# Row sums of an attention kernel gathered in two sets of heads instead of four, with a fourth sum tile and seven weight tiles

## The chip, the core and the metric

The program runs on one core of a Trainium2 chip. Its engines work side by side and meet only through semaphores: PE (TensorE, matmuls; PEld is its weight load), DVE (VectorE, elementwise work), ACT (ScalarE, activations, and here also copies out of PSUM), POOL (GpSimd, which here issues DMAs) and SP (SyncE, which issues most DMAs). The metric is the device time of the whole program in microseconds (us), lower is better. Before the change it is 1789.01 us, the median of three runs (1788.33 to 1789.2).

## What is computed

Two blocks work on the same 2048 tokens of width 1024 and are mixed by a gate for each token. Block A is attention with 32 heads of width 32; block B is a mixture of 64 small experts picked by product keys. The change touches block A only, and there the sum under the softmax:

```python
def _A_ref(x, wqkv, wo):
    qkv = (x @ wqkv) ...                      # q, k, v: 32 heads, 32 wide
    scores = einsum("bhqd,bhkd->bhqk", q, k) * (Dh ** -0.5)
    p = _softmax(scores, axis=-1)
    o = einsum("bhqk,bhkd->bhqd", p, v)
    return o.transpose(...).reshape(B, S, D) @ wo

g = sigmoid((x * gate_w).sum(-1, keepdims=True))
return g * a + (1 - g) * b
```

The kernel divides late. It multiplies the exponentials with V as they are, sums them over the keys beside that, and scales the heads' outputs by gate over sum ("scale factors") just before the product with `wo`.

## The kernel before

**Stages.** The first third computes q, k, the experts' scores and v. Attention follows, from about 606 to 1611 us. The product with `wo` and the experts' part end the program.

**Steps.** Attention runs over 32 heads (`H`) with 16 tiles of 128 keys each (`NT`); one tile of one head is a step, numbered `16 * head + tile`. A loop takes two steps at a time, as a batch: scores of two tiles on PE (`scores`, eight matmuls of 512 columns into a ring of seven PSUM banks), their exponentials on ACT into a tile P of 128 keys by 2048 queries, then the products P times V of the two tiles before (`pv`). After that come the functions that `at(step, ...)` has put down for these steps, and then `presum` of the two new tiles. The order on each engine's queue is this written order; SP and POOL too work their queues in order, so a DMA that waits holds what stands behind it.

**Where the sums come from.** A head's exponentials are summed over tiles first. DVE adds most tiles P into a sum tile `ACC[h]` (`presum`, L1449 and L1451). One tile of each head, `ACCD[h]`, takes up two or three others by accumulating DMAs that POOL issues (L1444). `merge` (L1454) adds both, five steps into the next head. That leaves 128 rows. For heads 0 to 27 accumulating DMAs from POOL fold them: `fold_half` to 64 rows, `fold_quarter` to 32, and for heads 0 to 23 `fold_eighth` to 16. `gather` (SP) moves the rows left to the head's place in a tile F of 128 rows. When a set of heads is complete (0 to 7, 8 to 15, 16 to 23 with 16 rows each, 24 to 27 with 32 each), `group_sums` does four matmuls with a selector (`sel8` or `sel`) into one ring bank, evicts them with ACT (L1484) and stores one row of sums per head with a DMA each (`smd<-ssb` in the profile). The heads 28 to 31 are summed by PE one by one (`head_sums`, and at the end L1739).

**Scale factors.** For each group of four heads `load_r` loads the sums (`rr<-smd`), `norm_r` makes their reciprocals and multiplies by the gate on DVE (L1517, L1518) and stores them (`rd<-rr`), all on SP's queue. `load_rb` later loads them spread out, for the first 256 tokens (`RB[0]`, tile `rb0`) and the next (`RB[1]`).

**Memory.** P has eight places, planned ahead in `p_places`: a place is held for 5 steps where DVE reads the tile and for 9 where a DMA does. A write to a place waits for the last reader of the tile that stood there. Four places lie in a pool on the left side of the memory, four on the right. `ACC` has three tiles, used in turn; the third shares its place with `vhl`, which is loaded near the end.

**The end of attention.** In head 31 (steps 496 to 511) `split_first` prepares the first operands of the product with `wo` on ACT and DVE between the exponentials and the sums. Then `merge(31)`, `rowsum` of head 31 (L1739) and its way through DRAM to the scale factors of the last group run, while PE does the products for which factors are there (`wo_mm`).

Of the kernel before, what the change touches and what calls it, by code (L numbers as in the profile page):

```python
# [9 lines left out]
F32 = mybir.dt.float32  # L10
# [3 lines left out]
OP = mybir.AluOpType  # L14
AX = mybir.AxisListType

S = 2048
D = 1024
H = 32
KC = D // 128  # L20
HC = KC // 2
NT = S // 128
# [9 lines left out]
def gated_mha_peer_kernel(ctx, tc, xT, wqkv, wv, wo, wq, k12, ug, v, out):  # L32
# [8 lines left out]
    nc = tc.nc  # L41
# [24 lines left out]
    ident = const.tile([128, 128], F32, name="ident")  # L66
    ones = const.tile([128, 32], F32, name="ones")
# [5 lines left out]
    warm = const.tile([128, 112], F32, name="fill")  # L73
# [4 lines left out]
    def dma(dst, src, queue=nc.sync):  # L78
        a, b = (ap.bitcast(F32) if ap.dtype == F32R else ap for ap in (dst, src))
        return queue.dma_start(a, b)  # L80
# [343 lines left out]
    for kc in range(KC):  # L424
# [12 lines left out]
        order = [(w, n, i) for w in range(2) for i in range(3) for n in range(2)]  # L437
        if kc == 0:
            order = [(w, n, i) for n in range(2) for pair in ((0, 2), (1,)) for w in range(2) for i in pair]
        if kc == KC - 1:  # L440
            order = [(w, n, i) for w in range(2) for n in range(2) for i in range(3)]
# [227 lines left out]
    wl_, wh_, pools = [], [], []  # L669
# [33 lines left out]
    sel = const.tile([128, KC * 4], F32, name="sel")  # L703
# [554 lines left out]
    P, pools = {}, {}  # L1258
# [2 lines left out]

    def p_places():

        due, last, order = list(range(-8, 0)), [0] * 8, []
        for k in range(H * NT):
            h, kt = divmod(k, NT)
            if kt != SUMS[h][0]:
                i = min(range(8), key=lambda j: due[j])
                due[i], last[i] = k + (9 if kt in SUMS[h] else 5), k
                order.append(i)  # L1270
        by_last = sorted(range(8), key=lambda j: last[j])
        return iter([by_last.index(i) for i in order])

    def p_tile(h, kt):

        i = next(pools["places"])
        P[h, kt] = pools["left" if i >= 4 else "right"].tile([128, S], F32, name=f"P{i}")
        return P[h, kt]

    def first_scores(*banks):  # L1280

        tp.close()
        pools.update(right=Pool("ppr", side="right"), places=p_places())
        K, Q = Z
        for kt, places in enumerate(banks):
            pt = p_tile(0, kt)
            for qc, i in enumerate(places):
                ps = ps1.tile([128, 512], F32, name=f"bk{i}")
                c = slice(qc * 512, (qc + 1) * 512)
                nc.tensor.matmul(ps, K[:98, kt * 128:(kt + 1) * 128], Q[:98, c], start=True, stop=True)  # L1290
                nc.scalar.activation(pt[:, c], ps, AF.Exp, scale=SCALE)
# [29 lines left out]
    ACC = {}  # L1321

    def new_acc(h):
        if h % 3 == 2 and h < H - 2:
            ACC[h] = keep.tile([128, S], F32, name="vhl")
        else:
            ACC[h] = wk.tile([128, S], F32, name=f"acc{h % 3 if h < H - 2 else h % 2}", bufs=1)

    def load_vhl(i):
        if i == 0:  # L1330
# [7 lines left out]
    wk = Pool("wk", bufs=2)  # L1338

    new_acc(0)  # L1340
    nc.vector.memset(sel, 0.0)
    for i in range(4):
        nc.vector.memset(sel[32 * i:32 * i + 32, i:i + 1], 1.0)
    sel8 = warm[:, :32]
    nc.vector.tensor_reduce(sel8[:, :8], ident.rearrange("p (j r) -> p j r", j=8), axis=AX.X, op=OP.max)
    nc.vector.memset(sel8[:, 8:], 0.0)
    vpool = Pool("vpool", bufs=2)
    kq = Pool("kq")
    pools["left"] = Pool("ppl")
# [7 lines left out]
    ring = pss.tile([128, NB, 512], F32, name="ring")  # L1357
# [3 lines left out]
    def ring_banks(n):  # L1361
        i = [(ring_no[0] + k) % NB for k in range(n)]
        ring_no[0] += n
        return i

    def on_ring(ins, *banks):

        for other, theirs in users:
            if ins.ins.engine != other.ins.engine and not theirs & set(banks):
                tc.declare_no_dep(ins.ins, other.ins, reason="different banks of the ring")  # L1370
        users.append((ins, set(banks)))
        del users[:-6 * NB]
# [56 lines left out]

    def rowsum(ps, *srcs, by=ones):
        for src in srcs:
            for qc in range(NQ):
                yield nc.tensor.matmul(ps[32 * qc:32 * qc + 32, :], by,
                                       src[:, qc * 512:(qc + 1) * 512],
                                       start=(src is srcs[0]), stop=(src is srcs[-1]))

    def presum(h, kt):
        sums = SUMS[h]  # L1440
        if kt == 0 or kt == sums[0] or (h == H - 1 and kt == NT - 1):
            return
        if kt in sums:
            nc.gpsimd.dma_start(ACCD[h], P[h, kt], accum_op=OP.add)  # L1444
            return
        if kt == min(set(range(1, NT)) - set(sums)):
            if h > 0:
                new_acc(h)
            nc.vector.tensor_add(ACC[h], P[h, 0], P[h, kt])  # L1449
        else:  # L1450
            nc.vector.tensor_add(ACC[h], ACC[h], P[h, kt])  # L1451
# [4 lines left out]
    F = {}  # L1456
# [7 lines left out]
    def fold_eighth(h):  # L1464
        nc.gpsimd.dma_start(ACC[h][:16], ACC[h][16:32], accum_op=OP.add)

    NE = 24

    def set_of(h):
        return (h // 8 * 8, 8) if h < NE else (NE, 4)  # L1470

    def gather(h):
        first, n = set_of(h)
        if h == first:
            F[first] = keep.tile([128, S], F32, name="rb0")
        rows, j = 128 // n, h - first
        dma(F[first][rows * j:rows * j + rows], ACC.pop(h)[:rows])

    def group_sums(first, n):
        i, = ring_banks(1)  # L1480
        for ins in rowsum(ring[:, i, :], F.pop(first), by=sel8 if n == 8 else sel):
            on_ring(ins, i)
        o = wk.tile([128, 512], F32, name="ssb")
        on_ring(nc.scalar.activation(o, ring[:, i, :], AF.Copy), i)  # L1484
        for j in range(n):
            g, r = divmod(first + j, 4)
            dma(SMD[g][r:r + 1, :].rearrange("o (q s) -> (o q) s", q=NQ), o[j::32, :])

    def head_sums(h):
        i, = ring_banks(1)  # L1490
        for ins in rowsum(ring[:, i, :], ACC.pop(h)):
            on_ring(ins, i)
        on_ring(norm_sums(h, ring[:, i, :]), i)
# [71 lines left out]
    def at(step, f, *a):  # L1565
        todo.setdefault(step, []).append((f, a))

    for h in range(H):
        base = h * NT
        g, j = divmod(h, 4)  # L1570
        if h < H - 1:
            at(base + NT, finish, h)
            at(base + NT + 5, merge, h)
            if h >= NP:
                at(base + NT + 8, head_sums, h)
            else:
                at(base + NT + 9, fold_half, h)
                first, n = set_of(h)
                if n == 8:
                    at(base + 2 * NT, fold_quarter, h)  # L1580
                    at(base + 2 * NT + 7, fold_eighth, h)
                    at(base + 2 * NT + 12, gather, h)
                else:
                    at(base + 2 * NT + 4, fold_quarter, h)
                    at(base + 2 * NT + 8, gather, h)
                if h == first + n - 1:
                    step = base + (3 * NT + 4 if n == 8 else 2 * NT + 14)
                    at(step, group_sums, first, n)
                    for i in range(n // 4):
                        at(step + 6 + 6 * i, load_r, first // 4 + i)  # L1590
                        at(step + 10 + 6 * i, norm_r, first // 4 + i)
        if h >= 1 and h + 1 < H:
            at(base + 2, load_head, h + 1)
        if g + 1 < G:
            at(base + 7, load_v, g + 1, j)
# [6 lines left out]
        at(30 * NT + 9 + i, load_vhl, i)  # L1602
    at(29 * NT + 13, load_o, 0, 0, 4)
    at(30 * NT + 7, load_o, 0, 4, KC - 1)
    at(30 * NT + 13, load_rb, 0, 0, KC - 1)
    at((H - 1) * NT + 8, load_rb, 1, 0, KC - 1)


    BT = 2
# [127 lines left out]
    load_t(2, [zp.tile([128, S], F32R, name="z1")], [fin.tile([128, S], F32R, name="t3l")])  # L1737
    sm = pso.tile([128, 512], F32, name="o")
    list(rowsum(sm, P[H - 1, NT - 1], ACC.pop(H - 1)))  # L1739
    split_hi(1)  # L1740
    for kc in range(1, KC - 1):
# [169 lines left out]
```

## Time and profile before

| | us |
|---|---|
| median of 3 runs | 1789.01 |
| lowest, highest | 1788.33, 1789.2 |
| the profiled execution | 1789.59 |
| its span, first to last instruction | 1787.5 |
| PE, ACT and DVE busy in the 100 us from 1000 | 100.00, 98.32, 91.40 |

A profile is one execution. Rows of a timeline give the start and the duration in us, the engine, the line, what is written from what, and how many instructions were merged into the row; in square brackets stands the idle time of the engine ahead of it and what ended that. "PEld" rows are weight loads, which stand ahead of their matmuls; "SPq" rows are DMAs being issued on SP, so their duration is that of the issue and not of the transfer. A row of the windows view gives, for a stretch, its length and for PE, PEld, DVE, ACT and POOL the busy time with the count of instructions, then the granted clock (1.00 throughout), the share of the DMA engines and GB/s. The granted clock of the whole execution is 1.0.

### The profile page before, as it was taken

How to read it: one execution, taken by the hardware profiler on the slowest of the kernel's cores; microseconds unless marked ns; L12 is line 12 of the kernel's file. 1: busy time of each engine (PE TensorE's matmuls, PEld its weight loads, DVE VectorE, ACT ScalarE, POOL GpSimd, SP SyncE). 2: the span in 40 equal slices, each digit the busy share in tenths (PEclk: the TensorE clock that was granted, in tenths of full speed). 3: DMA queues.
4: the chain of work that ended last, by engine and by line, in shares of the span. 5: the costliest groups of instructions: out<-in, count | busy, mean ns of one | idle time of the engine just before them, and what ended most of it. 6: DMA issues, size and time to landing. Idle time of an engine off the chain costs nothing.

```text
span 1787.5 us, 26063 instructions
## 1 busy us (share of the span) xinstructions
PE 1782.3 (100%) x9871; PEld 1090.3 (61%) x9871; DVE 1513.2 (85%) x1309; ACT 1307.3 (73%) x1705; POOL 297.3 (17%) x439
## 2 busy tenths in 40 slices
PE   9999999999999999999999999999999999999999
PEld 7777777888888644444444444444444444447887
DVE  8866876779997898989899998989989898887874
ACT  6545544532453699999999999999999999994221
POOL 1222222244213101111111111111111110000000
PEclk9999999999999999999999999999999999999999
DMA  8887687361348669899999999998989897888541
GB/s 286 315 310 267 223 311 294 131 210 58 113 174 293 210 142 200 173 197 183 176 206 194 199 191 203 194 189 197 191 188 195 189 196 173 198 190 300 205 160 59
DMA packets 120167, 361.17 MB, mean 202 GB/s; under 512 B 17800, under 2 KB 51864, under 8 KB 97320
## 3 DMA queue, kind: packets, MB, share of 16 engines
q0 software_dynamic: 31808, 160.76, 40.2%
q1 hardware_dynamic: 87456, 197.55, 35.6%
q8 instruction: 78, 1.28, 0.3%
q10 hardware_dynamic: 776, 1.19, 0.2%
q14 instruction: 49, 0.40, 0.1%
HBM read 173.04 MB, written 72.36 MB: 137 GB/s over the span
## 4 chain that ended last, share of the span: by engine, by line
PE 97%; DMA 1%; DVE 1%; issue 0%; ACT 0%; DVEq 0%; SPq 0%; ACTq 0%
PE ring L1402 29%; PE o L1423 26%; PE bk L304 15%; PE bk L987 7%; PE pa L987 7%; PE bk L729 5%; PE bk L292 2%; PE bk L346 2%; PE bk L1003 1%; PE pa L1662 1%; DVE acc L1451 1%; DMA wo_raw<-t0l 0%; PE bk L194 0%; DMA smd<-ssb 0%; DMA rb<-rd 0%
## 5 line engine op out<-in xcount | busy, mean ns | idle before, releaser
L1412 ACT ACTIVATE P<-ring 128x1024 f32<-128x1024 f32 (+2 forms) x1027 | 910.6, 987 | 16.7 <-PE ring L1402 0.6
L1451 DVE TENSOR_TENSOR acc<-acc,P 128x2048 f32<-128x2048 f32 x230 | 527.1, 2292 | 34.9 <-ACT P L1412 14.5
L1423 PE MATMUL o<-P,V 128*32 128x512 f32 x3840 | 464.8, 599 | 0.0
L1402 PE MATMUL ring<-Q,K 98*128 98x512 f32 x1024 | 272.3, 408 | 0.0
L1402 PEld LDWEIGHTS ring<-Q,K 98*128 98x128 f32 x1024 | 182.0, 188 | 144.6 <-ACT P L1412 80.3
L1402 PE MATMUL ring<-z,z 98*128 98x512 f32 x1016 | 269.5, 407 | 0.0
L1402 PEld LDWEIGHTS ring<-z,z 98*128 98x128 f32 x1016 | 180.8, 188 | 141.5 <-ACT P L1412 79.9
L1451 DVE TENSOR_TENSOR vhl<-vhl,P 128x2048 f32<-128x2048 f32 x104 | 238.3, 2292 | 17.7 <-ACT P L1412 8.3
L1423 PEld LDWEIGHTS o<-P,V 128*32 128x32 f32 x3840 | 98.8, 109 | 223.1 <-issue 213.7
L1444 POOL DMA_DIRECT2D accd<-P x81 | 72.1, 890 | 772.5 <-ACT P L1412 558.4
L304 PE MATMUL bk<-xh,A 128*128 128x512 f32 x336 | 81.9, 394 | 0.0
L304 PE MATMUL bk<-xh,S 128*128 128x512 f32 x336 | 81.0, 392 | 0.0
L304 PE MATMUL bk<-xl,S 128*128 128x512 f32 x336 | 79.7, 389 | 0.0
L304 PEld LDWEIGHTS bk<-xh,A 128*128 128x128 f32 x336 | 62.2, 188 | 22.0 <-issue 2.5
L139 ACT ACTIVATE hi<-u 128x512 fp32r<-128x512 f32 x42 | 26.5, 632 | 65.3 <-DVE u L520 35.6
L1449 DVE TENSOR_TENSOR acc<-P,P 128x2048 f32<-128x2048 f32 x22 | 50.4, 2292 | 26.9 <-ACT P L1412 26.8
L304 PEld LDWEIGHTS bk<-xl,S 128*128 128x128 f32 x336 | 63.0, 188 | 13.1
L304 PEld LDWEIGHTS bk<-xh,S 128*128 128x128 f32 x336 | 62.6, 188 | 12.9
L987 PE MATMUL pa<-woh,acc 128*128 128x512 f32 x216 | 70.0, 389 | 0.0
L1412 ACT ACTIVATE accd<-ring 128x1024 f32<-128x1024 f32 (+2 forms) x64 | 62.2, 1030 | 0.1
L520 DVE TENSOR_TENSOR u<-u,bk 128x512 f32<-128x512 f32 x70 | 46.6, 683 | 5.6 <-DMA wpd<-u 4.9
L1454 DVE TENSOR_TENSOR acc<-acc,accd 128x2048 f32<-128x2048 f32 x22 | 50.3, 2285 | 0.0
(329 smaller groups left out, 2323.0 us busy)
## 6 DMA issues: line engine op xcount, KB each, us to landing
accd<-P POOLq DMA_DIRECT2D x81, 1024.0 KB, 10.1
wqt<-in_wq SPq DMA_DIRECT2D x48, 512.0 KB
wraw<-in_wqkv SPq DMA_DIRECT2D x28, 512.0 KB
acc<-acc POOLq DMA_DIRECT2D x19, 512.0 KB, 12.1
kd<-hi POOLq DMA_DIRECT2D x32, 256.0 KB, 3.6
kd<-lo POOLq DMA_DIRECT2D x32, 256.0 KB, 5.6
qd<-hi POOLq DMA_DIRECT2D x32, 256.0 KB, 3.4
qd<-lo POOLq DMA_DIRECT2D x32, 256.0 KB, 3.5
```

Of the source, the lines that this page charges most:

```text
L292: nc.tensor.matmul(b0[w, n], AW[PLAIN[w, ki]][a][:, k, :], X[f"B{ki + 1}{n + 1}"][b][:, k, :], start=first, stop=last)
L304: nc.tensor.matmul(ps, a[i][:, k, :], b[j][:, k, :], start=(k == 0 and i == j == 0), stop=(k == HC - 1 and i == 1))
L520: nc.vector.tensor_tensor(out=out, in0=a, in1=b, op=OP.add)
L729: nc.tensor.matmul(ps, x_part(a, t // 4, kc)[:, tok], b, start=first, stop=last)
L987: nc.tensor.matmul(ps, self.a[a][i][:, k, :], self.b[b][j][k], start=(not first and k == 0 and i == j == 0), stop=(k == HC - 1 and i == 1))
L1402: on_ring(nc.tensor.matmul(ring[:, i, :], K[:98, kt * 128:(kt + 1) * 128], Q[:98, qc * 512:(qc + 1) * 512], start=True, stop=True), i)
L1412: on_ring(nc.scalar.activation(P[h, kt][:, q0 * 512:(q0 + m) * 512].rearrange("p (a m) -> p a m", a=m), ring[:, i:i + m, :], AF.Exp, scale ...
L1423: nc.tensor.matmul(O[h][32 * qc:32 * qc + 32, :], Vt[g][:, kt, 32 * j:32 * j + 32], p[:, qc * 512:(qc + 1) * 512], start=(kt == 0), stop=( ...
L1444: nc.gpsimd.dma_start(ACCD[h], P[h, kt], accum_op=OP.add)
L1449: nc.vector.tensor_add(ACC[h], P[h, 0], P[h, kt])
L1451: nc.vector.tensor_add(ACC[h], ACC[h], P[h, kt])
L1454: nc.vector.tensor_add(ACC[h], ACC[h], ACCD[h])
```

## The change

Heads 0 to 15 form one set, folded to 8 rows each, and heads 16 to 27 the other, where 16 to 23 are folded to 8 rows and 24 to 27 to 16. Each set is summed in one go with a selector of its own. A new fold, `fold_sixteenth`, makes 8 rows of 16. The sets are summed at steps 301 and 484 (before: 164, 292, 420 and 478), and the loads and norm steps of the groups follow in turn, six steps apart: at 307 to 329 for the four groups of the first set, and for the three of the second the loads at 490, 496 and 502 and the norm steps at 494, 500 and 506 (before, the last norm step of these was at 488). The loads of the scale factors for the first tokens follow suit: `RB[0]` in two parts, at steps 493 and 509, and `RB[1]` at 511 instead of 504.

`ACC` gets a fourth tile, `acc3`, in the left pool, and P has seven places instead of eight, three of them on the left.

```diff
     def p_places():
-        due, last, order = list(range(-8, 0)), [0] * 8, []
+        due, last, order = list(range(-7, 0)), [0] * 7, []
...
-                i = min(range(8), key=lambda j: due[j])
+                i = min(range(7), key=lambda j: due[j])
...
-        P[h, kt] = pools["left" if i >= 4 else "right"].tile([128, S], F32, name=f"P{i}")
+        P[h, kt] = pools["right" if i in (0, 1, 4, 5) else "left"].tile([128, S], F32, name=f"P{i}")
...
     def new_acc(h):
-        if h % 3 == 2 and h < H - 2:
+        i = h % 4 if h < H - 2 else 3 if h == H - 2 else 1
+        if i == 2:
             ACC[h] = keep.tile([128, S], F32, name="vhl")
+        elif i == 3:
+            ACC[h] = pools["left"].tile([128, S], F32, name="acc3")
         else:
-            ACC[h] = wk.tile([128, S], F32, name=f"acc{h % 3 if h < H - 2 else h % 2}", bufs=1)
+            ACC[h] = wk.tile([128, S], F32, name=f"acc{i}", bufs=1)
...
-    nc.vector.memset(sel, 0.0)
-    for i in range(4):
-        nc.vector.memset(sel[32 * i:32 * i + 32, i:i + 1], 1.0)
-    sel8 = warm[:, :32]
-    nc.vector.tensor_reduce(sel8[:, :8], ident.rearrange("p (j r) -> p j r", j=8), axis=AX.X, op=OP.max)
-    nc.vector.memset(sel8[:, 8:], 0.0)
+    SETS = {0: (16, [8] * 16), 16: (12, [8] * 8 + [16] * 4)}
+    by = {0: sel, 16: warm[:, :32]}
+    nc.vector.tensor_reduce(sel[:, :16], ident.rearrange("p (j r) -> p j r", r=8), axis=AX.X, op=OP.max)
+    nc.vector.tensor_copy(by[16][:, :8], sel[:, :8])
+    nc.vector.tensor_reduce(by[16][:, 8:12], ident[:, 64:].rearrange("p (j r) -> p j r", r=16), axis=AX.X, op=OP.max)
+    nc.vector.memset(sel[:, 16:], 0.0)
+    nc.vector.memset(by[16][:, 12:], 0.0)
...
+    def fold_sixteenth(h):
+        nc.gpsimd.dma_start(ACC[h][:8], ACC[h][8:16], accum_op=OP.add)
...
     def gather(h):
-        first, n = set_of(h)
+        first, (r0, n) = set_of(h), rows_of(h)
         if h == first:
             F[first] = keep.tile([128, S], F32, name="rb0")
-        rows, j = 128 // n, h - first
-        dma(F[first][rows * j:rows * j + rows], ACC.pop(h)[:rows])
+        dma(F[first][r0:r0 + n], ACC.pop(h)[:n])
...
-                if n == 8:
-                    at(base + 2 * NT, fold_quarter, h)
-                    at(base + 2 * NT + 7, fold_eighth, h)
-                    at(base + 2 * NT + 12, gather, h)
-                else:
-                    at(base + 2 * NT + 4, fold_quarter, h)
-                    at(base + 2 * NT + 8, gather, h)
+                folds = {32: {36: fold_quarter}, 16: {32: fold_quarter, 39: fold_eighth},
+                         8: {32: fold_quarter, 39: fold_eighth, 46: fold_sixteenth}}[rows]
+                for step, f in folds.items():
+                    at(base + step, f, h)
+                at(base + {32: 40, 16: 44, 8: 53}[rows], gather, h)
                 if h == first + n - 1:
-                    step = base + (3 * NT + 4 if n == 8 else 2 * NT + 14)
+                    step = base + {32: 46, 16: 52, 8: 61}[rows]
...
-    at(30 * NT + 13, load_rb, 0, 0, KC - 1)
-    at((H - 1) * NT + 8, load_rb, 1, 0, KC - 1)
+    at(30 * NT + 13, load_rb, 0, 0, 4)
+    at((H - 1) * NT + 13, load_rb, 0, 4, KC - 1)
+    at((H - 1) * NT + 15, load_rb, 1, 0, KC - 1)
```

In `at(base + ..., gather, h)` and the lines around it `base` is `16 * h`, so a head's own steps run from `base` to `base + 15`.

More of the change, by code (lines that the diff above doesn't have):

```diff
@@ L1267, in p_places @@
             if kt != SUMS[h][0]:
-                i = min(range(8), key=lambda j: due[j])
+                i = min(range(7), key=lambda j: due[j])
                 due[i], last[i] = k + (9 if kt in SUMS[h] else 5), k
                 order.append(i)
-        by_last = sorted(range(8), key=lambda j: last[j])
+        by_last = sorted(range(7), key=lambda j: last[j])
         return iter([by_last.index(i) for i in order])
@@ L1424, in pv, with rowsum @@
                              p[:, qc * 512:(qc + 1) * 512], start=(kt == 0), stop=(kt == NT - 1))
-    def rowsum(ps, *srcs, by=ones):
+    def rowsum(ps, *srcs, w=ones):
         for src in srcs:
             for qc in range(NQ):
-                yield nc.tensor.matmul(ps[32 * qc:32 * qc + 32, :], by,
+                yield nc.tensor.matmul(ps[32 * qc:32 * qc + 32, :], w,
                                        src[:, qc * 512:(qc + 1) * 512],
@@ L1465, in fold_eighth, with rows_of @@
         nc.gpsimd.dma_start(ACC[h][:16], ACC[h][16:32], accum_op=OP.add)
-    NE = 24
+    def fold_sixteenth(h):
+        nc.gpsimd.dma_start(ACC[h][:8], ACC[h][8:16], accum_op=OP.add)
     def set_of(h):
-        return (h // 8 * 8, 8) if h < NE else (NE, 4)
+        return max(f for f in SETS if f <= h)
+    def rows_of(h):
+        first = set_of(h)
+        rows = SETS[first][1]
+        return sum(rows[:h - first]), rows[h - first]
     def gather(h):
-        first, n = set_of(h)
+        first, (r0, n) = set_of(h), rows_of(h)
         if h == first:
             F[first] = keep.tile([128, S], F32, name="rb0")
-        rows, j = 128 // n, h - first
-        dma(F[first][rows * j:rows * j + rows], ACC.pop(h)[:rows])
+        dma(F[first][r0:r0 + n], ACC.pop(h)[:n])
     def group_sums(first, n):
         i, = ring_banks(1)
-        for ins in rowsum(ring[:, i, :], F.pop(first), by=sel8 if n == 8 else sel):
+        for ins in rowsum(ring[:, i, :], F.pop(first), w=by[first]):
             on_ring(ins, i)
@@ L1577, in gated_mha_peer_kernel @@
                 at(base + NT + 9, fold_half, h)
-                first, n = set_of(h)
-                if n == 8:
-                    at(base + 2 * NT, fold_quarter, h)
-                    at(base + 2 * NT + 7, fold_eighth, h)
-                    at(base + 2 * NT + 12, gather, h)
-                else:
-                    at(base + 2 * NT + 4, fold_quarter, h)
-                    at(base + 2 * NT + 8, gather, h)
+                rows, first = rows_of(h)[1], set_of(h)
+                n = SETS[first][0]
+                folds = {32: {36: fold_quarter}, 16: {32: fold_quarter, 39: fold_eighth},
[3 more added lines that the diff above has]
+                at(base + {32: 40, 16: 44, 8: 53}[rows], gather, h)
                 if h == first + n - 1:
-                    step = base + (3 * NT + 4 if n == 8 else 2 * NT + 14)
+                    step = base + {32: 46, 16: 52, 8: 61}[rows]
                     at(step, group_sums, first, n)
```

## The prediction

> **What bounds the kernel.** I read the page first, then one stretch of its windows, then the chain and short timelines. The page's busy table and chain come first; the third row (windows view) is 100 us of attention.
>
> ```profile
> PE 1782.3 (100%) x9871; PEld 1090.3 (61%) x9871; DVE 1513.2 (85%) x1309; ACT 1307.3 (73%) x1705; POOL 297.3 (17%) x439
> ...
> PE 97%; DMA 1%; DVE 1%; issue 0%; ACT 0%; DVEq 0%; SPq 0%; ACTq 0%
> ```
>
> ```profile
> 1000.00:1100.00 100.00, 100.00 (x619) 46.78 (x612) 91.40 (x41) 98.32 (x115) 16.91 (x20) 1.00 0.94 197
> ```
>
> PE carries 97% of the chain, but in attention ACT is at 98.3% and DVE at 91.4%, so time taken from PE counts only as far as the other two follow. The chain, in order of time, shows the beat:
>
> ```profile
> 918.86 2.07 PE ring L1402 x8
> 935.32 2.07 PE ring L1402 x8
> 943.13 2.07 PE ring L1402 x8
> ```
>
> Two batches of two tiles take 943.13 - 935.32 = 7.81 us, so a step (one tile) is 1.953 us. From 918.86 to 935.32 are 16.46 us, four batches (15.62) and 0.84 more. The PE timeline there shows what the extra is, and the views of lines L1435 and L1484 how often:
>
> ```profile
> 924.75 1.92 PE L1423 MATMUL o<-P,V 128*32 128x512 f32 x16
> 926.49 1.04 PE L1435 MATMUL ring<-rb,fill 128*32 128x512 f32 x8
> 927.46 1.89 PE L1402 MATMUL ring<-z,z 98*128 98x512 f32 x7
> ```
>
> ```profile
> L1435 PE MATMUL ring<-rb,fill x24: 592/592/592, 926.5 to 1428.8; 128*32 128x512 f32 x24
> ...
> L1435 PE MATMUL ring<-rb,sel x8: 592/592/592, 1543.4 to 1543.8; 128*32 128x512 f32 x8
> ```
>
> ```profile
> L1484 ACT ACTIVATE ssb<-ring x4: 597/599/602, 927.6 to 1544.5; 128x512 f32<-128x512 f32 x4
> ```
>
> Four group sums stand in the path (24 records and 8, eight to a set), each 0.84 to 0.85 us of PE: the attention part is set by PE.
>
> The end of head 31 is another matter. There DVE runs without a pause behind the exponentials and PE waits for it (DVE's timeline, then PEld's):
>
> ```profile
> 1585.13 2.29 DVE L1449 TENSOR_TENSOR acc<-P,P 128x2048 f32<-128x2048 f32 x1 [3.86 <-ACT P L1412]
> ...
> 1594.48 7.08 DVE L1451 TENSOR_TENSOR acc<-acc,P 128x2048 f32<-128x2048 f32 x3
> 1601.47 1.22 DVE L1561 TENSOR_TENSOR z<-wo_raw,z 128x1024 fp32r<-128x1024 f32 x1
> ...
> 1612.45 2.29 DVE L1454 TENSOR_TENSOR acc<-acc,accd 128x2048 f32<-128x2048 f32 x1
> ```
>
> ```profile
> 1614.80 0.16 PEld L1435 LDWEIGHTS o<-acc,ones 128*32 128x32 f32 x8 [0.92 <-DVE acc L1454]
> 1615.79 0.77 PEld L1655 LDWEIGHTS pa<-woh,z 128*128 128x128 f32 x4 [0.84 <-ACT z L1683]
> ```
>
> DVE last waits for ACT at 1585.13; the merge of head 31 ends at 1614.74, and PE's sums of that head start at 1614.80. What follows hangs on that merge: the sums' way through DRAM, and PE's one later gap:
>
> ```profile
> 1640.06 1.20 PE L1655 MATMUL pa<-woh,z 128*128 128x512 f32 x4 [0.39 <-ACT z L98]
> ```
>
> **The change, part by part.** (1) *Two group sums instead of four.* Eight matmuls (16 records) and two evictions of 599 ns go. On PE that is 2 x 0.85 = **-1.70 us** up to head 31. The two evictions free ACT, which is not what ends there.
>
> (2) *Scale factors later.* The norm step (L1517, L1518) of groups 4 to 6 moves: the set of heads 16 to 27 is summed at step 484, so these steps fall on 494, 500 and 506, and the last two lie in head 31 (496 on), where before there was none. Before, the last was at step 488, in head 30; its price is in DVE's timeline:
>
> ```profile
> 1559.29 7.08 DVE L1451 TENSOR_TENSOR acc<-acc,P 128x2048 f32<-128x2048 f32 x3
> 1566.29 0.54 DVE L1517 RECIPROCAL rr<-rr 128x64 f32<-128x64 f32 x1
> 1566.87 0.22 DVE L1518 TENSOR_TENSOR rr<-rr,G 128x64 f32<-128x64 f32 x1
> 1567.01 2.29 DVE L1451 TENSOR_TENSOR acc<-acc,P 128x2048 f32<-128x2048 f32 x1
> ```
>
> Three adds take 7.08, so they start (7.08 - 2.29) / 2 = 2.395 apart, 0.10 more than one lasts: each needs its forerunner's result. The third starts at 1564.08 and the next add at 1567.01, 2.93 later: between two adds a norm step costs 0.53, because part of it fills that gap. Step 500 stands between two adds: 0.53. Step 506 stands before the subtractions of step 507, which fill the gap already (it starts at 1601.47, 0.09 ahead of the last add's end at 1601.56), so it costs its whole 1566.29 to 1567.01 = 0.72. Together **+1.25 us** on DVE after 1585.13. The bounds are 0, if something slower hid them, and 2 x 0.76 = 1.5, the two bare durations. Nothing in the rows hides them, so I take 1.25. Head 30 has one norm step before and after, and 3.86 us idle behind it.
>
> So DVE starts head 31 1.70 earlier and ends it 1.70 - 1.25 = 0.45 earlier; PE, free 1.70 earlier, waits 1.25 for the merge, and the rest moves with that.
>
> (3) *Seven places for P.* A place is taken again after at least 6 steps where DVE reads it (8 places gave one more) and 10 where a DMA does. The tightest kind is tile 14 of head 19, which would take the place of tile 8. DVE's rows (adds of tiles 5 on, then tile 8 alone) and ACT's:
>
> ```profile
> 1212.30 23.85 DVE L1451 TENSOR_TENSOR acc<-acc,P 128x2048 f32<-128x2048 f32 x10
> ```
>
> ```profile
> 1219.48 2.29 DVE L1451 TENSOR_TENSOR acc<-acc,P 128x2048 f32<-128x2048 f32 x1
> ```
>
> ```profile
> 1225.79 0.60 ACT L1412 ACTIVATE P<-ring 128x512 f32<-128x512 f32 x1
> ```
>
> 1225.79 - 1221.77 = **4.0 us** to spare. For the DMAs (views of POOL on P and of L1465):
>
> ```profile
> DMA to landing us min/median/max: 6.9/10.1/14.7
> ```
>
> ```profile
> DMA to landing us min/median/max: 10.7/12.4/14.2
> ```
>
> Ten steps are 19.5 us; 2 us of exponentials and the longest landing, 14.7, leave about 2.8. Cost: 0. Without that cover a late reader stops ACT, and PE behind it, one for one.
>
> (4) *More folds.* 24 sixteenth folds and 4 more eighths go to POOL, which is 17% busy; the nearest row is the eighth fold's. The sixteenth is issued 7 steps (13.7 us) behind the eighth, so POOL waits at most 14.2 - 13.7 = 0.5 us for it, and the next accumulation queued behind it is 5 steps away: 0, at most 0.5 of the 2.8 above. Gathers shrink and come 7 steps behind the last fold instead of 5, and 8 steps before the matmuls as before: 0. A fourth sum tile leaves four heads for folds that end after 53 steps; 64 are there. The selectors, five small DVE instructions for seven ahead of the first head: 0, at most a few tenths either way.
>
> (5) *Sixteen stores in a row.* SP issues 16 stores of sums (then 12) where it issued 8, and the load of the factors stands behind them and behind head 20's K and Q. SP's rows, and DVE's where it waited for such a load:
>
> ```profile
> 919.91 0.39 SPq L80 DMA_DIRECT2D od<-osb  x1
> 920.40 1.61 SPq L80 DMA_DIRECT2D K<-kd  x2
> 922.06 1.14 SPq L80 DMA_DIRECT2D Q<-qd  x2
> 923.24 0.44 SPq L80 DMA_DIRECT2D Q<-shd  x1
> 928.22 5.75 SPq L80 DMA_DIRECT2D smd<-ssb  x8
> ```
>
> ```profile
> 1430.08 7.02 SPq L80 DMA_DIRECT2D smd<-ssb  x8
> ...
> 1438.43 1.34 SPq L80 DMA_DIRECT2D rr<-smd  x1
> ```
>
> ```profile
> 1449.30 0.55 DVE L1517 RECIPROCAL rr<-rr 128x64 f32<-128x64 f32 x1 [0.94 <-DMA rr<-smd]
> ```
>
> ```profile
> 1623.57 0.32 SPq L80 DMA_DIRECT2D rr<-smd  x1
> ```
>
> ```profile
> 1625.20 0.55 DVE L1517 RECIPROCAL rr<-rr 128x64 f32<-128x64 f32 x1 [2.26 <-DMA rr<-smd]
> ```
>
> Sixteen stores take 11.5 to 14.0 us and a head's output with the next loads 3.8 (919.91 to 923.68), so the factors' load is issued 15.3 to 17.8 after the first store. It lands 1.6 (1623.57 to 1625.20) to 10.9 us (1438.43 to 1449.30) later: at 16.9 to 28.7. DVE comes to the norm step of 311, ahead of tile 7's add, about 21.6 after that store: the store 1.6 behind the PV block of step 300 (1193.98), the add at 1212.30 + 2 x 2.395 = 1217.09, less 0.7 for the norm step that leaves tile 4 of this head, plus 0.85 for the sums in front. DVE thus waits 0 to 7.1 us. The load stands behind bulk transfers as the slow one did, so I take 7 us for the landing and a **wait of 2 us**. The 4.0 us of (3) cover that: 0 on PE. Above 4.0 each microsecond is lost, 3.1 at the upper end. [...]
>
> At step 494 twelve stores (8.6 to 10.5 us) stand ahead; DVE's idle 3.86 us in that head cover a wait. The last scale factors are loaded in two pieces from step 509, first needed by the products behind the merge: 0, at most about 1 if SP is held up behind them.
>
> **Sum.** -1.70 + 1.25 = **-0.45 us**. The profiled execution took 1789.59 (span 1787.5 and 2.1 around it), so 1789.1; it is 0.58 above the median, so against 1789.01 I say **1788.6 us**.
>
> **Rivals.** *The whole gain arrives*: if the norm steps hide in head 31, -1.70, 1787.3. For it: PE bounds 31 heads of 32. Against it: DVE has no idle there. Chance 0.17. *The factors' load in head 19 holds the places* (slower): a wait of 6 us is 2 us over the cover, 1788.6 + 2.0 = 1790.6; at 7.1, 1791.7. It turns slower than before from a wait of 4.4 us, a load that lands 26 us after the first store. For it: one landing in the trace took 10.9. Against it: the others kept DVE waiting less or not at all. Chance 0.20, and 0.06 that queues pile up beyond these rows to more than 8 us. *SP is late at the end*: +1, 1789.6, chance 0.08. *The sums were covered anyway* and nothing changes: 1789.0; against it are the 16.46 us. Chance 0.05. My own case has the remaining 0.44.
>
> **Numbers.** The range is 1787.0 to 1791.2: the full gain with 0.3 of scatter, and the rival with a 6.6 us wait. A measurement tells about 0.2% (3.6 us) from no change. Faster by that would need twice the whole gain: 0.03. Slower needs a wait above 8 us: 0.07. Within: 0.90.
>
> **What would show it.** Right: two extra pieces of 0.85 gone between heads 10 and 30; two reciprocals between 1583 and 1613, the merge of head 31 ending near 1614.3; PE's wait for it about 1.25 longer; the first reciprocal of the early set idle about 2 us for its load; score blocks on the 7.81 beat in heads 19 and 20. Wrong: score blocks there off the beat (the places), a merge 1.7 earlier (the full gain), or a PE gap at 1640 well above 0.39 (the end's loads).

## The result, and the profile after

The changed kernel takes **1808.83 us**, the median of six runs (1805.65 to 1812.71). The kernel before, run beside it, took 1789.11 (1788.33 to 1789.9). The ratio is 1.0109, with a 95% interval of 1.0096 to 1.0123: it is 1.1% slower, and the range given did not hold it. The profiled execution of the changed kernel took 1809.41 us, its span is 1807.6, which is 20.1 more than before.

The page's busy table and chain of the changed kernel answer to the two lines that opened the prediction:

```profile
PE 1784.4 (99%) x9855; PEld 1089.5 (60%) x9855; DVE 1512.9 (84%) x1307; ACT 1306.6 (72%) x1705; POOL 320.7 (18%) x467
...
PE 93%; DVE 3%; DMA 2%; issue 1%; SPq 1%; ACT 0%; DVEq 0%; ACTq 0%
```

PE runs 16 matmuls fewer, as the change says, and DVE, DMA and SP's queue take a larger part of the chain. The steady part is what it was (windows view, the same 100 us):

```profile
1000.00:1100.00 100.00, 100.00 (x613) 47.44 (x608) 91.46 (x41) 98.26 (x114) 17.88 (x23) 1.00 0.95 195
```

The loss sits in one place, head 19. Here are PE's timeline, ACT's and DVE's there. In the changed kernel scores are L1406, PV is L1427, exponentials L1416, adds L1455, the norm step L1526 and L1527.

```profile
1220.03 2.11 PE L1406 MATMUL ring<-Q,K 98*128 98x512 f32 x8
1222.07 1.92 PE L1427 MATMUL o<-P,V 128*32 128x512 f32 x16
1223.92 0.98 PE L1406 MATMUL ring<-Q,K 98*128 98x512 f32 x3
1240.77 2.77 PE L1406 MATMUL ring<-Q,K 98*128 98x512 f32 x5 [15.87 <-ACT P L1416]
1243.47 3.64 PE L1427 MATMUL o<-P,V 128*32 128x512 f32 x16
1247.04 2.14 PE L1406 MATMUL ring<-z,z 98*128 98x512 f32 x8
```

```profile
1239.70 1.94 ACT L1416 ACTIVATE P<-ring 128x1024 f32<-128x1024 f32 x2 [17.13 <-DVE acc L1455]
```

```profile
1236.59 0.55 DVE L1526 RECIPROCAL rr<-rr 128x64 f32<-128x64 f32 x1 [21.78 <-DMA rr<-smd]
1237.32 11.87 DVE L1455 TENSOR_TENSOR acc<-acc,P 128x2048 f32<-128x2048 f32 x5
...
1275.65 0.55 DVE L1526 RECIPROCAL rr<-rr 128x64 f32<-128x64 f32 x1 [4.42 <-DMA rr<-smd]
```

Read from the bottom up: DVE stands 21.78 us at the first norm step of the early set, because the factors have not landed. Its adds do not free the places of P, ACT stops 17.13, and PE 15.87. PE's losses can be taken from the starts. A block of eight score matmuls goes from 1220.03 to 1222.07, 2.04 us; the one begun at 1223.92 gives way to PV at 1243.47, 19.55 later: +17.51. The PV block behind it takes 3.57 (to 1247.04) where the one at 1222.07 took 1.85: +1.72. The wait of 4.42 in head 20 costs another 2.1 in the same way. Together 21.3; the two group sums give 1.70 back.

SP's timeline shows where the load was:

```profile
1193.46 15.46 SPq L80 DMA_DIRECT2D smd<-ssb  x16
1209.02 1.21 SPq L80 DMA_DIRECT2D od<-osb  x1
1210.33 2.63 SPq L80 DMA_DIRECT2D z<-kd  x2
1213.02 7.34 SPq L80 DMA_DIRECT2D z<-qd  x2
1220.41 0.45 SPq L80 DMA_DIRECT2D z<-shd  x1
1220.91 0.42 SPq L80 DMA_DIRECT2D rr<-smd  x1
```

The 16 stores take 15.46 us, head 18's output and head 20's K and Q (which go to tiles that the profile calls `z`) 11.9 up to 1220.91, and the load 15.7 from there to DVE's start at 1236.59. That is 43.1 us behind the first store, where I had 16.9 to 28.7. The chain of waits runs through the issue of K and Q and the load's 15.66. Ahead of 1210.45 it lies on PE, but SP's rows leave no gap above 0.1 us from the first store to the load.

At the end of attention (DVE's timeline, then PE's) nothing surprised:

```profile
1604.27 2.29 DVE L1453 TENSOR_TENSOR acc<-P,P 128x2048 f32<-128x2048 f32 x1 [4.49 <-ACT P L1416]
1606.48 0.55 DVE L1526 RECIPROCAL rr<-rr 128x64 f32<-128x64 f32 x1
...
1621.14 0.55 DVE L1526 RECIPROCAL rr<-rr 128x64 f32<-128x64 f32 x1
...
1632.84 2.29 DVE L1458 TENSOR_TENSOR acc<-acc,accd 128x2048 f32<-128x2048 f32 x1
```

```profile
1635.18 1.06 PE L1439 MATMUL o<-acc,ones 128*32 128x512 f32 x8 [1.22 <-DVE acc L1458]
```

From the first add of head 31 to the end of the merge are 1635.13 - 1604.27 = 30.86 us, against 1614.74 - 1585.13 = 29.61 before: +1.25, with the two norm steps inside. PE waits 1.22 for it. The terms add up: 21.3 - 1.70 + 1.22 - 0.39 (the later gap of PE at 1640, which is gone) = 20.4, where the spans differ by 20.1.

### The profile page after: what moved, and what is told of

It is laid out like the page before. It is cut to its first block, busy times and chain, and to the rows that moved or that the text cites. A ratio compares the mean times of both kernels' runs of the same rounds, so it can differ in the third digit from the quotient of the medians.

```text
span 1807.6 us, 26096 instructions
## 1 busy us (share of the span) xinstructions
PE 1784.4 (99%) x9855; PEld 1089.5 (60%) x9855; DVE 1512.9 (84%) x1307; ACT 1306.6 (72%) x1705; POOL 320.7 (18%) x467
## 4 chain that ended last, share of the span: by engine, by line
PE 93%; DVE 3%; DMA 2%; issue 1%; SPq 1%; ACT 0%; DVEq 0%; ACTq 0%
PE ring L1406 27%; PE o L1427 24%; PE bk L304 15%; PE pa L987 7%; PE bk L987 7%; PE bk L729 5%; PE bk L292 2%; DVE acc L1455 2%; PE bk L346 2%; DMA rr<-smd 2%; PE bk L1003 1%; PE pa L1671 1%; SPq L80 1%; PE pa L1664 0%; PE bk L194 0%
## 5 line engine op out<-in xcount | busy, mean ns | idle before, releaser
L1416 ACT ACTIVATE P<-ring 128x1024 f32<-128x1024 f32 (+2 forms) x1029 | 910.7, 983 | 37.9 <-DVE acc L1455 19.7
L1455 DVE TENSOR_TENSOR acc<-acc,P 128x2048 f32<-128x2048 f32 x264 | 604.9, 2291 | 35.0 <-ACT P L1416 11.5
L1427 PE MATMUL o<-P,V 128*32 128x512 f32 x3840 | 466.5, 601 | 0.0
L1406 PE MATMUL ring<-Q,K 98*128 98x512 f32 x1024 | 275.0, 409 | 16.9 <-ACT P L1416 16.9
L1406 PEld LDWEIGHTS ring<-Q,K 98*128 98x128 f32 x1024 | 182.3, 188 | 163.9 <-ACT P L1416 101.6
L1406 PE MATMUL ring<-z,z 98*128 98x512 f32 x1016 | 269.5, 407 | 0.0
L1406 PEld LDWEIGHTS ring<-z,z 98*128 98x128 f32 x1016 | 180.7, 188 | 142.5 <-ACT P L1416 78.4
L1427 PEld LDWEIGHTS o<-P,V 128*32 128x32 f32 x3840 | 99.0, 109 | 223.8 <-issue 214.4
L1455 DVE TENSOR_TENSOR vhl<-vhl,P 128x2048 f32<-128x2048 f32 x70 | 160.4, 2292 | 15.0 <-ACT P L1416 8.7
L1453 DVE TENSOR_TENSOR acc<-P,P 128x2048 f32<-128x2048 f32 x25 | 57.3, 2292 | 33.0 <-ACT P L1416 31.1
L304 PEld LDWEIGHTS bk<-xh,S 128*128 128x128 f32 x336 | 62.6, 188 | 12.9
L1416 ACT ACTIVATE accd<-ring 128x1024 f32<-128x1024 f32 (+2 forms) x64 | 62.1, 1029 | 0.1
L1458 DVE TENSOR_TENSOR acc<-acc,accd 128x2048 f32<-128x2048 f32 x25 | 57.1, 2285 | 0.0
## 6 DMA issues: line engine op xcount, KB each, us to landing
acc<-acc POOLq DMA_DIRECT2D x21, 512.0 KB, 10.9
```

Of the source, the lines that this page charges most:

```text
L304: nc.tensor.matmul(ps, a[i][:, k, :], b[j][:, k, :], start=(k == 0 and i == j == 0), stop=(k == HC - 1 and i == 1))
L1406: on_ring(nc.tensor.matmul(ring[:, i, :], K[:98, kt * 128:(kt + 1) * 128], Q[:98, qc * 512:(qc + 1) * 512], start=True, stop=True), i)
L1416: on_ring(nc.scalar.activation(P[h, kt][:, q0 * 512:(q0 + m) * 512].rearrange("p (a m) -> p a m", a=m), ring[:, i:i + m, :], AF.Exp, scale ...
L1427: nc.tensor.matmul(O[h][32 * qc:32 * qc + 32, :], Vt[g][:, kt, 32 * j:32 * j + 32], p[:, qc * 512:(qc + 1) * 512], start=(kt == 0), stop=( ...
L1458: nc.vector.tensor_add(ACC[h], ACC[h], ACCD[h])
```

## The experiments

The trace leaves two questions. Is it this one wait, and does the time come back when the wait goes? And why did the load take 43 us: sixteen stores where there were eight, the sixteenth folds, the seven places, or the rest of the DMA traffic? My first theory was the late load alone. In the diffs "..." stands for lines left out, and lines that only pass a tile on are not all shown.

**1. The norm steps later.** The norm steps of the early set and their later loads move 14 steps back (27 us); stores and places stay.

```diff
 for i in range(n // 4):
-    at(step + 6 + 6 * i, load_r, first // 4 + i)
-    at(step + 10 + 6 * i, norm_r, first // 4 + i)
+    late = 14 if first == 0 else 0
+    at(step + 6 + 6 * i + (late if i else 0), load_r, first // 4 + i)
+    at(step + 10 + 6 * i + late, norm_r, first // 4 + i)
```

> The changed kernel, with the first set's norm steps 14 steps (27.3 us) later and its loads of the second to fourth group with them; every store, fold, place and matmul stays. Theory 1 (DVE's wait of 21.8 us for the factors' load at step 311 is the whole loss; the places pass it on): the load still lands about 43 us after the first store, DVE comes to it at about 48.6, so it waits for nothing, no score block leaves the 3.907 us beat in heads 19 and 20, and the time is that of my sum, 1788.6 (1788.0 to 1789.2). Rival 2 (seven places or the sixteenth folds cost time by themselves): still 1795 or more. Rival 3 (the issue of 16 stores delays head 20's K and Q so that PE waits): still slower than 1800, with PE waiting for a DMA.

1807.77 us (1805.76 to 1808.8), ratio 1.01 [1.0085, 1.0115]. A plain miss for theory 1; rival 3 of the expectation names a part of what came. PE's and DVE's timelines show that the stall went elsewhere:

```profile
1233.94 3.75 PE L1406 MATMUL ring<-z,z 98*128 98x512 f32 x8 [5.68 <-DMA z<-qd]
1305.87 2.76 PE L1406 MATMUL ring<-Q,K 98*128 98x512 f32 x5 [10.46 <-ACT P L1416]
```

```profile
1277.49 0.55 DVE L1526 RECIPROCAL rr<-rr 128x64 f32<-128x64 f32 x1 [4.00 <-DMA rr<-smd]
1301.68 0.55 DVE L1526 RECIPROCAL rr<-rr 128x64 f32<-128x64 f32 x1 [11.91 <-DMA rr<-smd]
```

Head 19's norm step no longer waits. Instead PE waits 5.68 for the Q of head 20, which stands behind the same 16 stores (in the changed kernel, where DVE's longer wait holds PE up to 1240.77, its first scores with `z` begin at 1247.04 without a wait), and the third and fourth groups' loads come late in their turn. So there is a chain of late transfers, not one.

**2. The same, 5 steps later** (`late = 5`).

> As e1, but only 5 steps (9.8 us) later. Theory 1: DVE still waits, 21.8 - 9.8 = 12 us (8 to 16, since the runs of the changed kernel differ by 7 us among themselves); 4.0 of it are covered by the places, so PE loses 8 us and up to 4 more at the later norm steps: 1788.6 + 8 to 12 = 1797 to 1801. Theory 1 in a weaker form (DVE's wait costs PE in full, no cover): 1800 to 1804. Rival 2: as the changed kernel, 1808.8.

1799.64 us (1796.38 to 1801.19), ratio 1.0054 [1.004, 1.0069]: the size expected, but put together otherwise. DVE waits 14.6 and 3.3 for factors in heads 19 to 21, and PE 5.5 for Q.

**3. No sixteenth folds.** Rows 8 to 15 of each head are left out of its sums.

```diff
-                         8: {32: fold_quarter, 39: fold_eighth, 46: fold_sixteenth}}[rows]
+                         8: {32: fold_quarter, 39: fold_eighth}}[rows]
```

> The changed kernel without the 24 sixteenth folds; rows 8 to 15 of these heads are left out of the sums. If the folds of few rows clog the DMA engines (a packet of queue 0 took up to 4.6 us near 1212) and so delay the stores and the load (rival 4), the wait at step 311 falls below 8 us and the time to 1789 to 1793. If the order on SP's queue alone does it (theory 1 as it stands), the wait stays at 15 to 25 us and the time at 1804 to 1812.

1804.11 us (1803.81 to 1806.02), ratio 1.0086 [1.0072, 1.0101]. DVE still waits 18.23 at that norm step, so the added folds are not the main cause. They can be a part of it: the time is 4.7 below the changed kernel's, and the intervals of the two ratios overlap.

**4. The stores in runs of four.** Each group's stores stand 6 steps from the next, the first load right behind its four.

```diff
-        for j in range(n):
+    def store_sums(first, i):
+        for j in range(4 * i, 4 * i + 4):
...
+    at(step + 6 * i, store_sums, first, i)
-    at(step + 6 + 6 * i, load_r, first // 4 + i)
+    at(step + (2 if first == i == 0 else 6 + 6 * i), load_r, first // 4 + i)
```

> The changed kernel with the stores of a set in runs of four, one run for each group, 6 steps apart; the first factors' load stands 2 steps behind its four stores and ahead of head 20's loads, and no norm step moves. Theory 1 (the load is late because 16 stores and head 20's K and Q stand ahead of it): it is issued about 4 us after the first store and lands by 15, ahead of DVE's arrival at 21.4; the time is 1788.6 (1788.0 to 1789.2). If instead the DMA engines are too busy there for any small load (rival 4), it still lands late, DVE waits 5 to 15 us, and the time is 1792 to 1800.

1804.77 us (1795.73 to 1807.88), ratio 1.0069 [1.005, 1.0088]. The second miss, and the more telling one. The first norm step does not wait at all, the second and the fourth do; DVE's timeline, then SP's:

```profile
1215.26 0.54 DVE L1531 RECIPROCAL rr<-rr 128x64 f32<-128x64 f32 x1
1234.54 0.55 DVE L1531 RECIPROCAL rr<-rr 128x64 f32<-128x64 f32 x1 [6.70 <-DMA rr<-smd]
1244.47 0.55 DVE L1531 RECIPROCAL rr<-rr 128x64 f32<-128x64 f32 x1
1273.04 0.55 DVE L1531 RECIPROCAL rr<-rr 128x64 f32<-128x64 f32 x1 [16.37 <-DMA rr<-smd]
```

```profile
1248.00 0.61 SPq L80 DMA_DIRECT2D rd<-rr  x1
1261.65 0.36 SPq L80 DMA_DIRECT2D rr<-smd  x1
```

The `rr` tile has one buffer. The third group's factors leave it at 1248.00, SP then waits 12.9 us for that store to land, and the fourth load goes out at 1261.65; DVE has its factors at 1273.04, 11.4 later. The chain is therefore store, load, norm step, store, next load. The changed kernel's own chain of waits shows it as well: 6.84 us for that store and 8.84 for the load behind it, ahead of the wait of 4.42.

**5. All links loosened.** Stores in runs of four, four buffers for `rr`, and the early set's norm steps 20 steps later; the rest of the change stays.

```diff
-        R[g] = wk.tile([128, 128], F32, name="rr", bufs=1)[:, :64]
+        R[g] = wk.tile([128, 128], F32, name="rr", bufs=4)[:, :64]
...
+    at(step + 6 * i, store_sums, first, i)
     at(step + 6 + 6 * i, load_r, first // 4 + i)
-    at(step + 10 + 6 * i, norm_r, first // 4 + i)
+    at(step + (30 if first == 0 else 10) + 6 * i, norm_r, first // 4 + i)
```

> The changed kernel with all that could hold the first set's factors loosened: stores in runs of four, 6 steps apart; four buffers for the factors (0.5 KB each), so that a load no longer waits for the store of the group before; norm steps 24 steps (47 us) behind their loads. Sets, folds, places and the end stay. Theory 1, widened (every transfer of small rows is slow beside POOL's accumulations, and the chain load, norm step, store of four groups runs through one buffer in DVE's and SP's order): no wait of DVE for factors, no score block off the beat in heads 18 to 23, and the sum of the prediction holds, 1788.6 (1788.0 to 1789.3). If a cost is left that sits in the places or folds, 1790 to 1797 with PE or ACT waiting for DVE.

1788.38 us (1787.97 to 1788.9), ratio 0.9997 [0.9988, 1.0006]. No norm step of the early set waits and PE keeps its beat through heads 19 to 21. In all of attention PE waits once, at the end (waits view, 607 to 1650: us in total, times, longest):

```profile
PE o L1439 <- DVE acc L1458: 1.2, 1, 1.2
```

The whole loss is in these links.

**6. The end loosened as well.** In addition the late set's stores, loads and norm steps come one step apart, so that the norm steps fall on 496 to 498, ahead of head 31's first add. Against experiment 5:

```diff
-    at(step + 6 * i, store_sums, first, i)
-    at(step + 6 + 6 * i, load_r, first // 4 + i)
-    at(step + (30 if first == 0 else 10) + 6 * i, norm_r, first // 4 + i)
+    at(step + (6 * i if first == 0 else i), store_sums, first, i)
+    at(step + (6 + 6 * i if first == 0 else 6 + i), load_r, first // 4 + i)
+    at(step + (30 + 6 * i if first == 0 else 12 + i), norm_r, first // 4 + i)
```

> As e5, and the second set's loads one step apart at 490 to 492 and its norm steps at 496 to 498, ahead of DVE's first add of head 31, where DVE idles 3.9 to 4.5 us for ACT. If the two norm steps among the adds of head 31 cost 1.25 us at the end, as predicted, the merge of head 31 comes 1.25 earlier and the time is that of e5 less 1.25: 1787.3 (1786.9 to 1788.0), faster than before. If they cost nothing, the time is that of e5.

1787.33 us (1786.48 to 1787.92), ratio 0.999 [0.9981, 0.9999], 1.05 under experiment 5. DVE's timeline:

```profile
1583.53 2.29 DVE L1453 TENSOR_TENSOR acc<-P,P 128x2048 f32<-128x2048 f32 x1 [2.85 <-ACT P L1416]
...
1610.85 2.29 DVE L1458 TENSOR_TENSOR acc<-acc,accd 128x2048 f32<-128x2048 f32 x1
```

1613.14 - 1583.53 = 29.61, to the hundredth what it was before the change. The norm steps now lie in idle time that DVE has anyway. This version is the fastest of all, by 0.1%, with an interval that just leaves out no change.

**7. Seven places alone**, in the kernel before (in the change's own diff, the lines of `p_places` and the one that chooses the pool).

```diff
-        due, last, order = list(range(-8, 0)), [0] * 8, []
+        due, last, order = list(range(-7, 0)), [0] * 7, []
```

> The kernel before with seven places for P instead of eight and nothing else. Theory 1: the tightest place keeps 4.0 us, DVE never waits that long there, so 1789.0 as before (within 0.5). Rival 2 (the lost place costs by itself): slower by 2 us or more, with ACT waiting for DVE or a DMA before an exponential.

1788.6 us (1787.93 to 1789.12), ratio 0.9997 [0.9988, 1.0006]. In that kernel eight places were not needed: seven can pass a late reader on, but do not make one. How much of the late reader eight places would have covered in the changed kernel, no run shows.

**8. Without the accumulations of P on POOL**, in heads 18 to 20 alone; those tiles are left out of the sums. Sixteen stores, one buffer, the norm steps and seven places stay as the change has them.

```diff
+        if kt in sums and 18 <= h <= 20:
+            return
         if kt in sums:
             nc.gpsimd...
```

> The changed kernel without the accumulating DMAs of tiles P of heads 18 to 20 (these tiles are left out of the sums); stores, loads, folds and norm steps stay where they are. If POOL's accumulations (8 KB packets) are what slows the stores, K and Q and the factors' load, the 16 stores take 10 us or less, the first load lands within 28 us of the first store instead of 43, DVE waits 0 to 7 us at step 311 instead of 18 to 22, and the time is 1788 to 1793. If the order on SP's queue alone does it, the wait stays above 12 us and the time above 1797.

1788.58 us (1787.94 to 1789.5), ratio 0.9997 [0.9988, 1.0006]. SP's timeline, DVE's, and the windows view of 29 us in which all this happens, first of this kernel and then of the changed one:

```profile
1194.04 8.44 SPq L80 DMA_DIRECT2D smd<-ssb  x16
1202.59 0.39 SPq L80 DMA_DIRECT2D od<-osb  x1
1203.07 1.04 SPq L80 DMA_DIRECT2D z<-kd  x2
1204.16 1.17 SPq L80 DMA_DIRECT2D z<-qd  x2
1205.38 0.43 SPq L80 DMA_DIRECT2D z<-shd  x1
1205.86 0.36 SPq L80 DMA_DIRECT2D rr<-smd  x1
```

```profile
1215.31 0.54 DVE L1528 RECIPROCAL rr<-rr 128x64 f32<-128x64 f32 x1
```

```profile
1193.00:1222.00 29.00, 29.00 (x178) 14.05 (x175) 25.94 (x14) 28.29 (x35) 3.33 (x5) 1.00 0.57 127
```

```profile
1193.00:1222.00 29.00, 29.00 (x176) 14.01 (x174) 18.98 (x9) 28.67 (x35) 6.44 (x8) 1.00 0.85 149
```

Without them the same 16 stores take 8.44 instead of 15.46, Q 1.17 instead of 7.34, and DVE finds its factors there. The DMA engines' share falls from 0.85 to 0.57. The small transfers of SP's queue are late because of POOL's accumulations, by themselves or through the folds that stand behind them: in the changed kernel POOL issues two folds right behind an accumulation, at 1194.68 and 1196.62, beside the stores, and in the 29 us it is busy for 6.44 us there and for 3.33 here. The run does not tell the two apart; without the sixteenth folds alone (experiment 3) the stores still took 13.43.

**9. Sixteen stores in a row, the rest as in experiment 5.** Against that kernel:

```diff
-    def store_sums(first, i):
-        for j in range(4 * i, 4 * i + 4):
+        for j in range(n):
...
-    at(step + 6 * i, store_sums, first, i)
```

> e5 with the first set's 16 stores in one run again, ahead of head 20's K and Q; four buffers and late norm steps stay, so DVE waits for no factors. If the run of stores delays K and Q (in e1 PE waited 5.7 us for z<-qd), that wait is alone here: PE stalls once near 1226 by 5 to 8 us, and the time is 1788.4 + 5 to 8 = 1793 to 1797. If K and Q came late in e1 for another reason, 1788.4.

1796.12 us (1793.38 to 1797.51), ratio 1.004 [1.0025, 1.0054]: 7.7 above experiment 5. PE's timeline:

```profile
1234.06 3.75 PE L1406 MATMUL ring<-z,z 98*128 98x512 f32 x8 [5.46 <-DMA z<-qd]
1237.74 2.58 PE L1427 MATMUL o<-P,V 128*32 128x512 f32 x16
```

It is the delay of Q by itself: 5.46 of waiting, then 3.75 + 2.58 us where the blocks take 2.11 + 1.92 otherwise.

**10. Stores in fours and four buffers, the norm steps where the change has them.** Against experiment 5:

```diff
-    at(step + (30 if first == 0 else 10) + 6 * i, norm_r, first // 4 + i)
+    at(step + 10 + 6 * i, norm_r, first // 4 + i)
```

> e5 with the norm steps where the changed kernel has them, 4 steps behind their loads: stores in runs of four and four buffers alone. In e5 the four loads landed 13.6, 6.4, 3.6 and 10.7 us after their issue, the first and the last some 6 us after DVE would have come to them here. Theory 1: one or two waits of DVE of 3 to 9 us, of which the places cover 4.0, so 1788.4 + 0 to 8: 1789 to 1797. If a load that waits for no other is early enough, 1788.4.

1793.36 us, ratio 1.0022 [1.0012, 1.0033]. Nine of the ten runs lie between 1787.76 and 1796.95, with a median of 1793.06; the tenth took 3551.9, no trace shows why, and the ratio leaves it out. The profiled one (1788.85) had one wait of any size in head 19, in DVE's timeline:

```profile
1219.91 0.55 DVE L1531 RECIPROCAL rr<-rr 128x64 f32<-128x64 f32 x1 [4.76 <-DMA rr<-smd]
```

PE's beat slips by 0.27 there, so about 4.5 us of such a wait are covered. How the slower runs differ, no trace shows.

**11. The early set 7 steps later**, so that its sums and stores come behind head 20's K and Q.

```diff
-                    step = base + {32: 46, 16: 52, 8: 61}[rows]
+                    step = base + {32: 46, 16: 52, 8: 68}[rows]
```

> The changed kernel with the first set's sum 7 steps later, at step 308 (tile 4 of head 19, where the kernel before has its sums) with its loads and norm steps: 16 stores in one run, but behind head 20's K and Q instead of ahead. Theory 1: no wait for K and Q, and the first load has only stores ahead of it, so it lands 18 to 30 us after the first store where DVE comes after 18 to 21: a wait of 0 to 10 us and a loss of 0 to 6, plus up to 6 at the next three steps (one buffer): 1788.6 to 1800. If 16 stores in a row are what counts and their place does not, 1805 or more.

1803.94 us (1802.58 to 1804.93), ratio 1.0086 [1.0069, 1.0103], between what the two sides expected. SP's timeline and DVE's:

```profile
1209.41 17.44 SPq L80 DMA_DIRECT2D smd<-ssb  x16
...
1232.61 1.04 SPq L80 DMA_DIRECT2D rr<-smd  x1
```

```profile
1235.85 0.55 DVE L1526 RECIPROCAL rr<-rr 128x64 f32<-128x64 f32 x1 [7.11 <-DMA rr<-smd]
1248.67 0.55 DVE L1526 RECIPROCAL rr<-rr 128x64 f32<-128x64 f32 x1 [5.21 <-DMA rr<-smd]
1271.15 0.55 DVE L1526 RECIPROCAL rr<-rr 128x64 f32<-128x64 f32 x1 [7.87 <-DMA rr<-smd]
```

Q is in time and PE no longer waits for it, but the stores take as long as ever, and one wait becomes three shorter ones, of which PE sees none, 2.82 and 7.29 us. Another order of the same transfers brought back 4.9 us of 20 here, with the stores at 17.44.

## Why the prediction was wrong, point by point

**Step (1) was right.** Two sums of 0.85 us are left on PE below head 28 instead of four. Experiment 6, which takes away what the change adds elsewhere, ends at 1787.33, where the full gain was put at 1787.3. That it is so close is in part luck: the interval of its ratio allows a gain of 0.2 to 3.4 us.

**Step (2) was right**, 1.25 us to the hundredth; that it is added work and nothing else is shown by experiment 6, where it goes. PE's wait for the merge, 1.22, is what was forecast within 0.03.

**Steps (3) and (4) were right in what they cost**: places nothing by themselves (experiment 7), folds nothing that could be told once the links are loose (experiment 5); beside late transfers they may cost some us (experiment 3). The cover of 4.0 us is about 4.5: experiment 10, and 21.78 - 17.13 = 4.65 between DVE's wait and ACT's in the changed kernel.

**The step that failed is (5), "Sixteen stores in a row", with its "wait of 2 us", bounds 0 to 7.1.** The mechanism named there, and priced as the rival "The factors' load in head 19 holds the places", is what happened; the size was 21.78. DVE's arrival was right, 21.35 us behind the first store against about 21.6. All three durations up to the load's landing were too small: the stores 15.46 (I had 11.5 to 14.0), output and next K and Q 11.9 (3.8), the landing 15.7 (1.6 to 10.9). I took the rows of eight stores, of K and Q and of a load each from where it stood in the trace of before, and set them one behind the other as if each kept its price elsewhere. The trace of before has K and Q of this same head 20, with no stores ahead of them (SP's timeline):

```profile
1205.19 1.06 SPq L80 DMA_DIRECT2D z<-kd  x2
1206.30 1.16 SPq L80 DMA_DIRECT2D z<-qd  x2
```

Behind the 16 stores they took 2.63 and 7.34. What raises these prices comes with POOL's accumulations: without them the stores took 8.44, K and Q 1.04 and 1.17 (experiment 8). Such accumulations were in the trace of before, issued at 1195.67 and 1208.72, and the DMA engines' share from 1193 to 1222 was 0.98 there, where it is 0.85 in the changed kernel; so the share alone does not tell the price. The moment counts as well: before, K and Q went out at 1205.19, and POOL issues nothing between 1199.17 and 1208.72; in the changed kernel they went out at 1210.33, behind POOL's issues at 1207.39 and 1207.95. In experiment 4 they went out at 1205.58 and took 1.04 and 1.18.

Taking 11.5 as 15.5 alone would not have been enough. The rest is in links that the prediction did not follow. The loads of the later groups wait for the one buffer, which I did not name as a wait (experiment 4). K and Q of head 20 stand behind the stores, which I counted for the factors' load but not for PE (5.5 us, experiments 1 and 9). And PE, once it has stood, runs at a clock of 0.50 for 6.2 us (below). My rival charged one microsecond for each microsecond above the cover: 21.78 - 4.0 = 17.8 for head 19, where the starts give 17.51 + 1.72 = 19.2.

**What stays open:** how POOL's accumulations slow the rows of SP's queue, which no run here shows; why a run of 16 stores takes 13 us in one kernel and 17 in the next (13.43 in experiment 3, 17.44 in 11); and why the times of experiments 4 and 10 scatter over 9 to 12 us.

## What to carry to other kernels

In this kernel a small DMA has no price of its own: the 16 stores took from 8.44 us (experiment 8) to 17.44 (experiment 11). Read such a row together with what the other queues move in the same stretch, and when a change puts it elsewhere, take the price from there or leave the bound open. Follow a late transfer past its first waiter, to what stands behind it on its queue and to the buffer that it must free: here removing one wait (experiments 1 and 4) brought back 1 and 4 us of 20, and loosening all links brought back all. Gathering small work into fewer, larger sets saved 1.70 us as planned, and cost 21 until the sets' transfers had slack.

## What the hardware showed beyond that

In head 19 PE's granted clock falls to 0.50 while PE stands, and it stays there for 6.2 us after work returns. Two stretches of the windows view of the changed kernel:

```profile
1240.00:1247.00 7.00, 6.23 (x21) 1.89 (x21) 6.69 (x4) 5.47 (x7) 0.00 (x0) 0.50 0.27 73
1247.00:1251.00 4.00, 4.00 (x29) 1.88 (x25) 3.96 (x4) 3.31 (x4) 0.00 (x0) 1.00 0.00 0
```

PE resumes at 1240.77 and runs at 0.50 until 1247, 21 matmuls in 6.2 us. The score block with the stall in it has 0.98 + 2.77 = 3.75 us of matmul time instead of 2.11, the PV block 3.64 instead of 1.92: 3.4 us on top of 15.87 of waiting. In experiment 9 a wait of only 5.46 cost 2.3 more in this way, with the clock at 0.50 from 1234 to 1239.

The fall came soon after PE stood: its last matmul ends at 1224.90, the clock is 1.00 up to 1226.5 and 0.50 from 1226.6 on, 1.6 to 1.7 us later. In experiment 11 the 16 PV matmuls behind a wait of only 2.82 us took 3.64 us instead of 1.92, as long as at the half clock here. The clock of those few us is not shown; the mean of that execution is 0.996. So even a wait of 2.82 us was followed by slow matmuls in this case.
